# Twelve unused products in two stops of TensorE, ahead of the first job's scores

## The chip, the core and the metric

The kernel runs on one core of one Trainium2 chip. The metric is the device time of one execution in microseconds (us); the time given is the median of 8 runs. One execution was also profiled: the profile lists each instruction with its engine, start and length. TensorE (PE) does matrix products, with its weight loads listed apart (PEld); VectorE (DVE) does elementwise work, ScalarE (ACT) activations and copies, GpSimd (POOL) little here, and SyncE (SP) issues most of the DMA transfers.

## What is computed

Two layers, one after the other, in float32: a retention attention without softmax over 8 batches, 8 heads, 576 positions and 64 dimensions, and a gated feed-forward layer over its 4608 rows of 512.

```python
def _attn_ref(q, k, v):
    B, H, S, D_ = q.shape
    scale = 1.0 / np.sqrt(D_)
    scores = scale * np.matmul(q, k.transpose(0, 1, 3, 2))
    gamma = 1.0 - 2.0 ** (-5.0 - np.arange(H, dtype=np.float32))
    pos = np.arange(S)
    rel = pos[:, None] - pos[None, :]
    Dmat = np.where(rel >= 0, gamma[:, None, None] ** rel[None, :, :], 0.0)
    return np.matmul(scores * Dmat[None, :, :, :], v)

# x: the heads side by side, (4608, 512)
def _moe_ref(x, w_gate, w_val, w_out, rms_g):
    rms = np.sqrt(np.mean(x * x, axis=-1, keepdims=True) + 1e-06)
    xn = x / rms * rms_g
    g = xn @ w_gate
    silu = g * (1.0 / (1.0 + np.exp(-g)))
    return (silu * (xn @ w_val)) @ w_out
```

## The kernel before

The attention is cut into 32 jobs, one for each batch and pair of heads. A job handles its sequence in chunks of 64 positions. `scores` (L276) multiplies k and q inside a chunk, `states` (L296) multiplies k and v of a chunk into a 64 x 64 state for each head, `weigh` (L309) applies the causal mask to the scores on VectorE, `sums` (L323) adds the states up along the sequence on VectorE, `values` (L348) multiplies the weighted scores with v, and `carried` (L369) adds what the summed states give. `slot(j)` (L404) puts these in order: the values of job j-1, the scores and states of job j, its weighing and sums, and then the carried part of job j-1. The feed-forward part takes 384 rows at a time; the first two such units use plain products (`up_plain`, L602), the others a seven-product scheme for 2 x 2 blocks.

The order of every engine's instructions is written out by hand: the program runs under a manual schedule, so each engine does its instructions in the order in which the code below emits them, and semaphores hold it where data or a buffer is not yet there.

`start` (L905) is the part around the change. It makes the identity matrix and a tile of ones, runs six products of the ones with themselves into a bank named `warm` (L918 to L920), issues the first weight chunk and three tables on ScalarE's queue, and then the loads of the first eight jobs on SyncE's queue (`load_first`, L149, with `load_tails`, L189, for the last 64 positions). Then come `turn(0)`, `scale_v(0)` and three activations of the weights' conversion (`act(3)`), and a loop over eight jobs. In each turn of the loop stand `slot(j)`, `turn(j + 1)` for the next job, and `scale_v` of a later job, with pieces of the weight conversion between them.

`turn(j)` (L220) brings q and k of a job into transposed form. On TensorE it runs 8 products for q (L234, tile `turn_q`), 4 transposes for k (L228, `turn_k`) and 2 for the tails (L242, `turn_t`); on ScalarE it copies the results to `qT` and `kT` (L239, L248). `scale_v` (L259) scales the four pieces of v on ScalarE (L264). The scores need `qT` and `kT`, the states the scaled v.

The products write to banks of PSUM, of which the pool `banks` rotates five; `bank(name)` takes the next one. A float32 product appears in the trace as two matrix records and two weight loads; a transpose as one.

Of the kernel before, what the change touches and what calls it, by code (L numbers as in the profile page):

```python
# [14 lines left out]
P = 128  # L15
# [7 lines left out]
def _decay_tables(H, D):  # L23

    pairs = _gamma(H).reshape(H // 2, 2).T
    rows = np.repeat(pairs, D, axis=0)
    pos = np.arange(L)
    p = np.concatenate([pos, pos])  # L30
    gq = rows[:, :, None] ** (pos + L) / np.sqrt(D)
    t = pairs.T[None] ** -p[:, None, None], rows**L, gq, np.roll(gq, D, axis=0)
    return [np.ascontiguousarray(x).astype(np.float32) for x in t]


def _causal_table():

    return np.ascontiguousarray(np.tile(np.triu(np.ones((L, L), np.float32)), (2, 1)))
# [3 lines left out]
def kernel(  # L42
# [11 lines left out]
    nc = tc.nc  # L54
# [33 lines left out]
    def bank(name):  # L88
        return banks.tile([P, 512], F32, tag="b", name=name)
# [9 lines left out]
    ones = const.tile([P, P], F32, name="ones")  # L99
# [72 lines left out]
    def find_places():  # L172

        n = NFULL * 2 * D
        kv = {
            nm: [raw.tile([P, n], F32, tag=nm, name=f"first_{nm}_{i}", bufs=bufs) for i in range(bufs)]
            for nm, bufs in (("k", 4), ("v", 3))
        }
        other = raw.tile([P, S], F32, tag="qraw", name="first_k_7")[:, :n]
        sums = [ffn.tile([P, 3 * 2 * HU], F32, tag=t, name=f"first_{t}") for t in ("sums", "t1")]  # L180
        room = h_of[0].rearrange("p f t -> p (f t)")[:, 2 * NHP * 4 * P :]
        more = w_up[1][:, 8:].rearrange("p b f -> p (b f)")[:, 6 * DM :]
        return {
            "k": kv["k"] + kv["v"] + [other],
            "v": [t[:, i * n : i * n + n] for t in sums for i in range(2)]
            + [more[:, i * n : i * n + n] for i in range(3)] + [room],
        }
# [29 lines left out]
            out=t, in_=v[b, 2 * hp : 2 * hp + 2, NFULL * P :].rearrange("e p d -> p e d")  # L217
        )

    def turn(j):  # L220

        d = st[j]
        last = bank(f"turn_{j}_t")
        for nm in "qk":
            ps = bank(f"turn_{j}_{nm}")
            for c in range(NFULL):
                if nm == "k":
                    nc.tensor.transpose(  # L228
                        out=ps[:, c * P : c * P + P],
                        in_=d["k"][:, c].rearrange("p e d -> p (e d)"), identity=ident,  # L230
                    )
                    continue
                for e in range(2):
                    nc.tensor.matmul(  # L234
                        ps[side(e), c::NFULL], lhsT=d["q"][:, e, c], rhs=ident,
                        start=True, stop=True,
                    )
            t = d[nm + "T"] = att.tile([P, S], F32, tag=nm + "T", name=f"{nm}T_{j}")
            nc.scalar.copy(out=t[:, : NFULL * P], in_=ps)  # L239
        for i, nm in enumerate("qk"):  # L240
            o = slice(i * TAIL, i * TAIL + TAIL)
            nc.tensor.transpose(  # L242
                out=last[:, o], in_=d[nm + "t"].rearrange("p e d -> p (e d)"),
                identity=ident[:TAIL, :TAIL],
            )
        for i, nm in enumerate("qk"):
            o = slice(i * TAIL, i * TAIL + TAIL)
            nc.scalar.copy(out=d[nm + "T"][:, NFULL * P :], in_=last[:, o])  # L248
# [10 lines left out]
    def scale_v(j):  # L259
        d = st[j]  # L260
        hp = jobs[j][1]
        for e in range(2):
            for t in (d["v"][:, :, e], d["vt"][:, e]):
                nc.scalar.activation(  # L264
                    out=t, in_=t, func=AF.Copy, scale=gv[: t.shape[0], hp, e : e + 1]
                )
# [4 lines left out]
    def side(i):  # L271
        return slice(i * L, i * L + L)
# [489 lines left out]
    for g in range(NG):  # L762
        for m, src in enumerate((moe_w_gate, moe_w_val)):
            for half in range(2):
                n = (half * NH + 2 * g) * P
# [31 lines left out]
    def load_chunks(n, queue=nc.scalar):  # L797

        nonlocal n_loads
        while n_loads < min(n, len(chunks)) and waits_at.get(spare(n_loads)) is None:  # L800
            load_chunk(n_loads, queue)
            n_loads += 1
# [90 lines left out]
    def weights(n):  # L893

        for _ in range(n):
            next(steps, None)
# [8 lines left out]
    def start():  # L905

        h_of[0] = ffn.tile([P, NF, U], F32, tag="h", name="h_0")
        tables = list(zip((causal, gv, gc, gq, gx), (_causal_table(), *_decay_tables(H, D))))

        def table(i, queue):  # L910
            t, values_ = tables[i]
            src = nc.inline_tensor(values_, name=t.tensor.name + "_table")
            queue.dma_start(out=t, in_=src.ap())

        make_identity(nc, ident)
        nc.scalar.activation(out=tick, in_=mhalf[:1], func=AF.Silu)
        nc.vector.memset(ones, 1.0)
        warm = bank("warm")  # L918
        for _ in range(6):
            nc.tensor.matmul(warm[:, :P], lhsT=ones, rhs=ones, start=True, stop=True)  # L920
        first_places.update(find_places())
        load_chunks(1)
        for i in (1, 0, 2):
            table(i, nc.scalar)
        weights(3)
        for j in range(2 * NHP):
            load_first(j, {0: range(2), 1: range(2, H), NHP: range(H)}.get(j))
            if j == 1:
                table(3, nc.sync)
            load_chunks((1, 1, 1, 1, 2, 2, 2, 3)[j], nc.sync)  # L930
        table(4, nc.sync)
        nc.sync.dma_start(out=rms_g, in_=moe_rms_g.rearrange("(c p) -> p c", p=P))
        load_chunks(4, nc.sync)
        turn(0)
        scale_v(0)
        act(3)
        squares = []
        for j in range(2 * NHP):
            slot(j)
            if j + 1 < 2 * NHP:  # L940
                turn(j + 1)
            if squares:
                gather(*squares.pop())
            for i in ((1,), (2,), (3,), (4, 5), (6,), (7,), (), ())[j]:
                scale_v(i)
            if j:
                u, c = divmod(j - 1, NHP)
                squares.append((u, c, square(u, c)))
            act(1)
            if j == 5:  # L950
                norm_1(0)
            elif j == 6:
                norm_2(0)
            weights((2, 0, 0, 1, 1, 1, 1, 0)[j])
            if j == 4:
                gather(*squares.pop())
            elif j == 5:
                diagonals(0)
            act(1)
        gather(*squares.pop())  # L960
        load_qk(2 * NHP)
        load_kv(2 * NHP)
        made = combine_out()
        for m, g in [(m, g) for g in range(NG) for m in range(2)]:
            for u in range(2):
                weights_to(4 * g + 2 * m + 1)
                for i, _ in enumerate(up_plain(u, m, g)):
                    if not (u or m or g):
                        if i == 0:
                            values(2 * NHP - 1)  # L970
                            carried(2 * NHP - 1)
                            gather(1, NHP - 1, square(1, NHP - 1))
                        elif i == 1:
                            norm_1(1)
                        elif i == 2:
                            diagonals(1)
                        elif i == 3:
                            norm_2(1)
                    weights(2)
                    act(1)  # L980
                    if u and m and g == NG - 1:
                        weights_to(len(chunks))
                        next(made, None)
                    if i == 1:
                        weights_to(4 * g + 2 * m + 2)
        for _ in made:
            pass
        for blk, t in first_blocks.items():
            keep(blk, t)
        rest = across(1)  # L990
        next(rest)
        following(2 * NHP - 1)
        for i, _ in enumerate(rest):
            if i == 1:
                norm_0(2)
                differences(0)
            elif i == 2:
                norm_1(2)
                diagonals(2)
            elif i == 4:  # L1000
                norm_2(2)
        rest = across(0)
        next(rest)
        combine(1)
        slot(8, rest=False)
        following(8)
        for _ in rest:
            pass
        combine(0)
        slot(9)  # L1010
        following(9)
# [18 lines left out]
    with tc.manual_schedule():  # L1030
# [4 lines left out]
        for u in range(2, NU):  # L1035
# [11 lines left out]
            for i, _ in enumerate(rest):  # L1047
                if i == 0 and turns:
                    prepare_next(turns.pop())
                if i == 2:  # L1050
                    behind(u, 6)
                    at, n = SLOTS[u % 3]
# [33 lines left out]
```

## Time and profile before

| what | value |
|---|---|
| median of 8 runs | 1141.37 us |
| lowest and highest of them | 1139.93 and 1142.92 us |
| the profiled execution | 1140.38 us |
| its span, first to last instruction | 1138.6 us |
| mean granted TensorE clock | 0.997 |
| first job's q, turned on TensorE | 4.07 to 6.05 us |
| first job's k, turned on TensorE | 8.18 to 8.81 us |
| first job's scores begin | 10.05 us |
| last load in the chain of waits lands | 42.7 us |
| feed-forward products without a break from | 67.4 us |

Times inside the execution are counted from its first instruction. The page lists the busy time of each engine, the span in 40 slices, the queues, and the chain of work that ended last, followed back from the last instruction. A timeline lists instructions of one kind in order of time, merged where they follow each other, and in brackets the idle time of the engine ahead of them with what ended it. The granted clock is the share of TensorE's full clock that the records show; where there is no record yet, 1.0 is printed.

### The profile page before, as it was taken

The numbers are of one execution on the slowest core, as the hardware profiler recorded it, in microseconds if no ns is written. First come the engines' busy times: TensorE is split into PE (matmuls) and PEld (weight loads), VectorE is DVE, ScalarE is ACT, GpSimd is POOL, SyncE is SP. The second block draws the span as 40 slices with busy tenths as digits, with TensorE's granted clock in tenths as the row PEclk, the third lists the DMA queues.
The fourth block names the chain that finished last, engine by engine and source line by source line (L and its number), as shares of the span: only waits on it lengthen the run. The fifth ranks groups of instructions, "written<-read, shape, count | busy, mean of one in ns | idle before, by whom it ended". The sixth has DMA issues, their size and how long they took to land.

```text
span 1138.6 us, 24713 instructions
## 1 busy us (share of the span) xinstructions
PE 1116.4 (98%) x10470; PEld 1044.3 (92%) x10470; DVE 726.8 (64%) x1431; ACT 258.4 (23%) x508; POOL 39.7 (3%) x64
## 2 busy tenths in 40 slices
PE   7899999999999999999999999999999999999998
PEld 6655557999999999999999999999999999999998
DVE  5788868655675685375767676465676666446352
ACT  5546642012212211211221121121121220120210
POOL 0000000470000000000000000000000000000000
PEclk9999999999999999999999999999999999999999
DMA  8764336335364474053454555215436503303304
GB/s 203 215 184 148 111 126 197 62 64 135 96 136 98 112 160 143 1 121 88 106 125 60 132 133 120 114 35 118 119 79 141 142 20 97 126 1 100 124 1 111
DMA packets 292942, 125.40 MB, mean 110 GB/s; under 512 B 270432, under 2 KB 275808, under 8 KB 292832
## 3 DMA queue, kind: packets, MB, share of 16 engines
q1 hardware_dynamic: 282688, 107.66, 38.1%
q10 hardware_dynamic: 10144, 16.16, 4.4%
q8 instruction: 82, 1.34, 0.5%
q14 instruction: 28, 0.23, 0.1%
HBM read 108.83 MB, written 14.94 MB: 109 GB/s over the span
## 4 chain that ended last, share of the span: by engine, by line
PE 93%; SPq 3%; DVE 2%; DMA 1%; issue 1%; ACT 0%; DVEq 0%; POOL 0%; POOLq 0%
PE w L557 14%; PE x L557 14%; PE z L557 13%; PE up L614 10%; PE xo L688 8%; PE wo L688 8%; PE zo L688 8%; PE y L557 7%; PE yo L688 4%; SPq L165 2%; PE av L355 2%; PE s L284 1%; PE av L377 1%; PE s L304 1%; DVE sum L333 1%
## 5 line engine op out<-in xcount | busy, mean ns | idle before, releaser
L581 ACT COPY m<-x 128x384 f32<-128x384 f32 x60 | 28.7, 478 | 338.4 <-PE x L557 338.4
L688 PE MATMUL xo<-h,w_out 128*128 128x192 f32 x528 | 90.3, 328 | 0.0
L557 PE MATMUL w<-sums,w_val 128*128 128x192 f32 x480 | 88.7, 328 | 0.3
L557 PE MATMUL x<-x,w_val 128*128 128x192 f32 x480 | 88.8, 328 | 0.0
L557 PE MATMUL z<-x,w_gate 128*128 128x192 f32 x480 | 87.9, 326 | 0.7 <-DVE u L564 0.7
L557 PE MATMUL x<-x,w_gate 128*128 128x192 f32 x480 | 88.6, 328 | 0.0
L557 PE MATMUL z<-x,w_val 128*128 128x192 f32 x480 | 87.9, 326 | 0.0
L557 PE MATMUL w<-sums,w_gate 128*128 128x192 f32 x480 | 87.8, 326 | 0.0
L688 PEld LDWEIGHTS xo<-h,w_out 128*128 128x128 f32 x528 | 85.9, 190 | 0.6
L688 PE MATMUL wo<-h,w_out 128*128 128x192 f32 x504 | 85.3, 326 | 0.0
L564 DVE TENSOR_TENSOR u<-m,y 128x384 f32<-128x384 f32 x60 | 33.1, 552 | 79.0 <-PE y L557 79.0
L688 PEld LDWEIGHTS wo<-h,w_out 128*128 128x128 f32 x504 | 82.5, 190 | 0.0
L557 PEld LDWEIGHTS w<-sums,w_val 128*128 128x128 f32 x480 | 79.2, 190 | 2.7 <-DVE c L564 2.7
L557 PEld LDWEIGHTS z<-x,w_gate 128*128 128x128 f32 x480 | 79.6, 190 | 1.0 <-issue 1.0
L557 PEld LDWEIGHTS x<-x,w_gate 128*128 128x128 f32 x480 | 79.3, 190 | 0.5
L557 PEld LDWEIGHTS x<-x,w_val 128*128 128x128 f32 x480 | 79.2, 190 | 0.6
L557 PEld LDWEIGHTS z<-x,w_val 128*128 128x128 f32 x480 | 79.7, 190 | 0.0
L557 PEld LDWEIGHTS w<-sums,w_gate 128*128 128x128 f32 x480 | 79.6, 190 | 0.0
L564 DVE TENSOR_TENSOR h<-u,w 128x384 f32<-128x384 f32 x60 | 33.1, 551 | 69.5 <-PE w L557 69.4
L576 ACT ACTIVATE h<-h 128x384 f32<-128x384 f32 x90 | 47.0, 522 | 89.6 <-DVE h L564 89.6
L614 PE MATMUL up<-x,w_gate 128*128 128x384 f32 x192 | 63.3, 488 | 0.9 <-DVE x L526 0.7
L614 PE MATMUL up<-x,w_val 128*128 128x384 f32 x192 | 62.4, 486 | 0.0
(187 smaller groups left out, 1766.3 us busy)
## 6 DMA issues: line engine op xcount, KB each, us to landing
w_out<-w_blocks SPq DMA_DIRECT2D x70, 768.0 KB, 5.1
out_dram<-o SPq DMA_DIRECT2D x368, 24.0 KB, 1.6
qraw<-in_q_dram SPq DMA_DIRECT2D x96, 72.0 KB, 2.7
kraw<-in_k_dram SPq DMA_DIRECT2D x96, 72.0 KB, 2.7
k<-in_k_dram SPq DMA_DIRECT2D x48, 128.0 KB, 2.9
v<-in_v_dram SPq DMA_DIRECT2D x48, 128.0 KB, 2.9
w_out<-in_moe_w_gate_dram ACTq DMA_DIRECT2D x5, 1024.0 KB, 5.8
w_out<-in_moe_w_out_dram ACTq DMA_DIRECT2D x3, 1024.0 KB, 4.8
```

Of the source, the lines that this page charges most:

```text
L165: nc.sync.dma_start(out=t[:, :, e], in_=src[b, 2 * hp + e, : NFULL * P].rearrange("(c p) d -> p c d", p=P),)
L284: nc.tensor.matmul(s[side(odd), e, i * L : i * L + L], lhsT=d["kT"][side(e), c * L : c * L + L], rhs=d["qT"][side(e), c * L : c * L + L], ...
L304: nc.tensor.matmul(o[side(e)], lhsT=d["k"][side(odd), i, e], rhs=d["v"][side(odd), i, e], start=True, stop=True,)
L333: nc.vector.scalar_tensor_tensor(out=t[:, c], in0=t[:, c - 1], scalar=gc[:, hp : hp + 1], in1=part, op0=ALU.mult, op1=ALU.add,)
L355: mm = nc.tensor.matmul(av[odd][column(j, odd, e), i * L : i * L + L], lhsT=d["v"][side(odd), i, e] if c < NC - 1 else d["vt"][:, e], rhs= ...
L377: mm = nc.tensor.matmul(av[odd][column(j, odd, e), i * L : i * L + L], lhsT=d["sum"][side(e), c - 1], rhs=d["qT"][side(e), c * L : c * L + L],
L557: nc.tensor.matmul(ps[:, i * HU : i * HU + HU], lhsT=w_up[m][:, 2 * blk + c, cut], rhs=t_of[u][blk][:, c], start=(start and i == c == 0), ...
L564: nc.vector.tensor_tensor(out=o, in0=a, in1=pairs_of(ps), op=ALU.add)
L576: nc.scalar.activation(out=o, in_=c, func=AF.Silu)
L581: nc.scalar.copy(out=s1, in_=pairs_of(x_))
L614: nc.tensor.matmul(ps[:, :U], lhsT=w_up[m][:, 4 * half + c, i * P : i * P + P], rhs=x_of[u][:, c], start=(c == 0), stop=(c == NHP - 1),)
L688: nc.tensor.matmul(ps[:, i * HU : i * HU + HU], lhsT=a[:, c, i * P : i * P + P], rhs=rhs[:, c], start=(start and i == c == 0), stop=False, ...
```

## The change

The six products at the start become a call of a new helper, `warm_up(n)`, which emits n products of the tile of ones with itself into the same bank. `turn` gets an argument `waits` with two counts: so many such products ahead of the transposes of k, and so many after the transposes of the tails. Only `turn(0)` passes counts, 8 and 4; all other calls use 0 and 0. The results of these products are not read. The emitted order on the other engines is the same.

```diff
-    def turn(j):
+    warm_of = {}
+
+    def warm_up(n):
+
+        if not warm_of:
+            warm_of[0] = bank("warm")
+        for _ in range(n):
+            nc.tensor.matmul(
+                warm_of[0][:, :P], lhsT=ones, rhs=ones, start=True, stop=True
+            )
+
+    def turn(j, waits=(0, 0)):
+
 
         d = st[j]
         last = bank(f"turn_{j}_t")
         for nm in "qk":
+            if nm == "k":
+                warm_up(waits[0])
             ps = bank(f"turn_{j}_{nm}")
...
                 identity=ident[:TAIL, :TAIL],
             )
+        warm_up(waits[1])
         for i, nm in enumerate("qk"):
...
-        warm = bank("warm")
-        for _ in range(6):
-            nc.tensor.matmul(warm[:, :P], lhsT=ones, rhs=ones, start=True, stop=True)
+        warm_up(6)
         first_places.update(find_places())
...
-        turn(0)
+        turn(0, (8, 4))
         scale_v(0)
```

## The prediction

> **What bounds the kernel now.** I read the page's busy shares first, then the chain of waits over the first 66 us, then the timeline of the first 20 us engine by engine, and last the clock by windows. Busy shares with the slices say that TensorE is the bound of almost the whole run, and that only the start leaves it room:
>
> ```profile
> PE 1116.4 (98%) x10470; PEld 1044.3 (92%) x10470; DVE 726.8 (64%) x1431; ACT 258.4 (23%) x508; POOL 39.7 (3%) x64
> ...
> PE   7899999999999999999999999999999999999998
> ```
>
> From 67.4 us on the chain is TensorE almost alone, so an earlier end needs an earlier arrival there. The chain of waits (start, length, what) tells how the start is paced:
>
> ```profile
> 3.69 5.52 DMA first_sums<-in_v_dram
> 9.22 0.41 SPq L165
> ...
> 38.61 4.09 DMA w_val<-in_v_dram
> 42.72 0.75 ACT w_val L264 x2
> 43.47 0.42 ACT sq L439
> 43.92 0.56 DVE sq L449
> ...
> 67.40 5.40 PE up L614 x16
> ```
>
> SyncE issues loads from 0.73 to 38.6 us, a last one lands at 42.7, then VectorE works almost without a gap to 66 us, then TensorE. No product of the first job stands in it. The timeline around the two stops (start, length, engine, line, operation, out<-in, count, idle time before and what ended it):
>
> ```profile
> 4.07 1.98 PE L234 MATMUL turn_q<-ident,h 128*64 128x128 f32 x16
> 8.18 0.63 PE L228 MATMUL turn_k<-ident,first_k 128*128 128x128 f32 x4 [2.13 <-DMA first_k<-in_k_dram]
> 8.74 0.33 PE L242 MATMUL turn_t<-ident,w_val 64*128 64x64 f32 x2
> 9.40 0.59 ACT L239 COPY kT<-turn_k 128x512 f32<-128x512 f32 x1
> 10.05 1.34 PE L284 MATMUL s<-qT,kT 64*64 64x64 f32 x40 [0.98 <-ACT kT L239]
> 12.45 0.89 DVE L316 SCALAR_TENSOR_TENSOR ret<-s,causal 128x320 f32<-128x320 f32 x2 [3.16 <-PE last L304]
> 17.41 0.35 ACT L264 ACTIVATE w_val<-w_val,gv 64x64 f32<-64x64 f32 x1 [0.93 <-DMA w_val<-in_v_dram]
> 18.21 0.62 PE L304 MATMUL s<-first_sums,first_k 64*64 64x64 f32 x25 [1.35 <-ACT first_sums L264]
> 18.92 0.89 DVE L316 SCALAR_TENSOR_TENSOR ret<-s,causal 128x320 f32<-128x320 f32 x2 [0.78 <-PE last L304]
> ```
>
> TensorE stops twice, 2.1 us for the first k and about 1 us for the copies of ScalarE. The last three lines matter most: at 17.41 ScalarE, at 18.21 TensorE and at 18.92 VectorE all stand idle in the second job for one load. The windows (stretch, length, busy PE, granted clock, DMA share, GB/s) show what the stops cost:
>
> ```profile
> 6.32:9.73 3.41, 0.89 (x6) 0.99 0.98 151
> 9.73:13.15 3.42, 3.10 (x80) 0.51 1.08 237
> 13.15:16.56 3.41, 2.97 (x95) 1.00 1.13 196
> 37.04:40.45 3.41, 1.99 (x43) 1.00 0.81 195
> ```
>
> After a stretch with 0.89 us of work the clock is halved for one stretch of 3.41 us, and the first scores and states fall into it. A stretch with 1.99 us of work kept the clock.
>
> **What the Trainium skill says.** "TensorE: Matmul & The Clock Gate", Part 1, gives the gate half and full rate alone, decided per free-running window of 3413 ns: an idle one halves the clock, a busy one restores it. The trace agrees: the slow stretch is 3.41 us at 0.50, behind a nearly idle one of the same length. The same page's specification table calls the queues of ScalarE and VectorE strict FIFO; here the copies and scalings of ScalarE do run in the order written, and the argument below rests on it. "DMA: Bandwidth & Descriptors", Why small descriptors are slow, explains dear small packets; here the first 62 us move 28241 packets, 23180 of them under 512 B, and the DMA engines are near full at 8 to 18 us.
>
> **The change, part by part.** It adds 12 products and removes and moves nothing else; the orders of VectorE, ScalarE, GpSimd and SyncE are the same with the same waits. No DMA is added. The products read a constant and write their own bank, and carry no wait.
>
> Price of one: the six at the start are 12 records in 2.93 us at half rate. Taking one record's latency, about 0.46 us, off leaves 11 steps of 0.224 us, so 0.45 us a product, 0.22 us at full clock (an estimate by the halving). The start does run at half rate although the page prints 1.0 there: its turn_q takes 1.98 us, the later ones at full clock 1.09 us.
>
> First stop, 8 products, 16 records. TensorE can issue from about 5.7 us (turn_q's end at 6.05 less the latency). Up to 6.32 at half rate: 0.62/0.224 = 2.8 records. The other 13.2 at 0.112 = 1.5 us: the last ends near 8.1. The first k lets TensorE go at 8.15, so they fit, to within 0.1 us. Behind them wait turn_k and turn_t, and behind those ScalarE's kT copy at 9.40, for which turn_k was ready at 8.81: 0.59 us more of cover. Cost zero; without cover it would be their 1.5 to 3.6 us (all at full, all at half rate).
>
> Second stop, 4 products, 8 records of 0.112 = 0.9 us from about 8.9 us, ended by about 10.0; the scores start at 10.05. Cost zero, 0.1 us at most.
>
> What it gives locally: the stretch from 6.32 to 9.73 holds about 0.9 + 1.7 + 0.8 = 3.4 us instead of 0.89, so the clock stays up from 9.73 to 13.15. The scores take 0.78 us as at 15.93 instead of 1.34. The states can't follow at once: the second head's v is scaled on ScalarE until 11.25 (10.74 + 0.51). From there the second job's states took 0.69 us at full clock (18.21 to 18.90), so they end at about 11.97 instead of 12.42. VectorE weighs the first job at 12.0 instead of 12.45: 0.45 us earlier. The second turn_q saves another 0.34 us (1.43 less 1.09).
>
> Where that goes: TensorE's values of the first job wait at 15.41 for ScalarE's copy of the second qT, which stands behind three 1.15 us activations of the weights (11.38 to 14.89), none of them waiting for TensorE. From 15.41 TensorE is where it was. ScalarE goes on to 16.48, and stands until the v tails of the second job, issued by SyncE at 12.20, land at 17.4. Hence states at 18.21, and VectorE's weighing at 18.92, unmoved: its 0.45 us turns into idle time, 0.78 + 0.45 = 1.23 us before that line. After it all five engines are where they were. If the load came earlier by the whole 0.93 us, ScalarE would be the next late one, not TensorE. Sum: 0 - 0 + 0 = 0 us on the end, against the profiled execution's 1140.38 us (span 1138.6 and 1.8 around it), which lies 1.0 us under the median. So 1141.4 for the median.
>
> One side effect: with earlier work the stretch 13.15 to 16.56 empties. Left in it are some turn_k and turn_t (0.6 us), four products of the values (0.3) and 15.41 to 16.56 (1.15): about 2.0 us, and 1.99 us kept the clock above. I take no loss; a halved stretch to 19.97 with its 2.06 us of work would cost 1 to 2 us locally.
>
> **The rivals.**
> Gain carried (faster). A halved clock over 3.10 us of work loses 1.55 us; if the start were paced by TensorE after all in most executions, all of that would be won: 1139.8; with two stretches halved in other executions, 3.1 us: 1138.3. For it: the records do show the loss, and one execution says little on the window's phase in others. Against: the idle times at 17.41, 18.21 and 18.92, and again VectorE's 0.96 us at 35.09 and ScalarE's 1.57 us at 37.50, both for loads.
>
> Late first scores (slower). The extra products hold up turn_k, if the array is still at half clock over the first stop. Then 16 x 0.224 = 3.6 us from 5.7 us end at 9.3, turn_k at about 10.3, kT's copy 0.9 us late; turn_t to 10.4, then 8 x 0.224 = 1.8 us, so scores at 12.3 instead of 10.05 and the first weighing 2.3 us late. 0.78 us idle before 18.92 takes some: 1.5 us late there, 1142.9 if no later load wait absorbs it, and 2.3 us if the first doesn't either: 1143.7. It decides from where the products end after 8.7 us (8.15 + 0.59). For it: the fit is tight and the phase free. Against: a clock record of 1.0 from 6.32, and turn_k at 8.18 as quick (0.63 us) as at 20.78 (0.66).
>
> No change of clock. In the execution's phase the gate halves anyway, or had not halved: 1141.4 too, since the products are hidden.
>
> **How the numbers follow.** Forecast 0.71, gain carried 0.15, late scores 0.08, no change of clock 0.06. What this kernel's measurement can tell from no change is about 0.2%, 2.3 us. Of the gain's 0.15 I put 0.09 beyond that, since only the two-stretch value passes it, and 0.02 of the forecast for drift; of the late scores 0.05 and 0.01 for drift: faster 0.11, slower 0.06, same 0.83. Range: the runs before span 1139.9 to 1142.9; reaching to the one-stretch gain (1139.8) and the absorbed lateness (1142.9), trimmed to what two in ten leave out: 1139.3 to 1142.7.
>
> **What would show it.** Right: clock 1.0 from 9.73 to 13.15, scores still at about 10.05 but 0.8 us long, the first weighing near 12.0, TensorE's wait at 15.4 and the second weighing at 18.9 unmoved, the second's idle time up to about 1.2 us, the up products still at 67.4. Wrong: turn_k later than 8.3, scores later than 10.2, a halved stretch after 13.15, or a second weighing before 18.5.

## The result and the profile after

The changed kernel takes 1146.95 us (median of 10 runs, 1145.49 to 1148.73) against 1141.13 us (28 runs). The ratio is 1.0051, 95% interval 1.0042 to 1.006: 5.8 us slower, outside the range given. The profiled execution took 1146.99 us, its span is 1145.2 us.

TensorE's busy time and the clock row of the page of the changed kernel:

```profile
PE 1123.5 (98%) x10494; PEld 1050.7 (92%) x10494; DVE 726.9 (63%) x1431; ACT 258.4 (23%) x508; POOL 40.1 (3%) x64
...
PEclk8899999999999999999999999999999999999999
```

TensorE has 24 matrix records more (10494 against 10470) but is busy 7.1 us longer, and the first two slices of the clock row, which showed 9 (90% of full clock or more), show 8. The chain of waits of the same execution (start, length, what) shows where the time sits:

```profile
17.57 1.01 PE s L319 x25
...
20.40 1.90 PE turn_q L248 x16
...
32.71 3.28 issue
...
73.37 5.40 PE up L629 x16
```

Where the chain before ran through SyncE's issues, it now runs through TensorE: `turn_q` of the third job takes 1.90 us where it took 1.09, and for 3.28 us TensorE runs nothing ("issue" is time in which the engine waits for nothing that the profile shows). The unbroken feed-forward products begin at 73.37 us instead of 67.40: of the 6.6 us between the two profiled executions, 6.0 are lost before that.

The timeline of the two stops and of VectorE's weighings says when (the columns as before):

```profile
5.98 2.32 PE L227 MATMUL warm<-ones 128*128 128x128 f32 x16
8.14 0.60 PE L242 MATMUL turn_k<-ident,first_k 128*128 128x128 f32 x4
8.93 1.16 PE L227 MATMUL warm<-ones 128*128 128x128 f32 x8
10.02 0.81 PE L299 MATMUL s<-qT,kT 64*64 64x64 f32 x40
11.87 0.89 DVE L331 SCALAR_TENSOR_TENSOR ret<-s,causal 128x320 f32<-128x320 f32 x2 [2.60 <-PE last L319]
18.72 0.89 DVE L331 SCALAR_TENSOR_TENSOR ret<-s,causal 128x320 f32<-128x320 f32 x2 [1.15 <-PE last L319]
26.05 0.89 DVE L331 SCALAR_TENSOR_TENSOR ret<-s,causal 128x320 f32<-128x320 f32 x2 [3.16 <-PE s L319]
32.18 0.89 DVE L331 SCALAR_TENSOR_TENSOR ret<-s,causal 128x320 f32<-128x320 f32 x2 [1.97 <-PE s L319]
43.77 0.89 DVE L331 SCALAR_TENSOR_TENSOR ret<-s,causal 128x320 f32<-128x320 f32 x2 [5.10 <-PE s L319]
```

Up to the second job all is as predicted, even a little early. The weighings of the third to fifth job stood so before:

```profile
24.14 0.89 DVE L316 SCALAR_TENSOR_TENSOR ret<-s,causal 128x320 f32<-128x320 f32 x2 [1.05 <-PE s L304]
29.51 0.89 DVE L316 SCALAR_TENSOR_TENSOR ret<-s,causal 128x320 f32<-128x320 f32 x2 [1.20 <-PE s L304]
36.51 0.89 DVE L316 SCALAR_TENSOR_TENSOR ret<-s,causal 128x320 f32<-128x320 f32 x2 [0.72 <-PE s L304]
```

Now they are 1.9, 2.7 and 7.3 us late. Two things lie there. The windows of the changed kernel (stretch, length, busy PE, PEld, DVE, ACT, POOL, clock, DMA share, GB/s) show two stretches at half clock, each twice as long as the one before and in places where TensorE is needed:

```profile
13.40:16.81 3.41, 2.18 (x81) 1.77 (x80) 3.13 (x8) 2.96 (x8) 0.09 (x1) 1.00 0.64 140
16.81:23.64 6.83, 6.07 (x84) 5.22 (x84) 4.61 (x15) 1.78 (x5) 0.00 (x0) 0.50 0.99 230
33.60:37.00 3.40, 1.01 (x22) 0.94 (x23) 1.99 (x8) 0.00 (x0) 0.00 (x0) 1.00 1.09 224
37.29:44.12 6.83, 5.96 (x133) 4.92 (x129) 1.73 (x5) 5.39 (x14) 0.09 (x1) 0.50 1.04 240
```

The first follows the stretch that the earlier work left emptier, the second follows the long gap. And the gaps put down to "issue" have a place of their own, which shows when TensorE's records are counted: matrix records, weight loads and the semaphore instructions between them, in order of their start, the first as number 0. A gap "after record 1217" stands ahead of the record with that number.

### The profile page after: what moved, and what is told of

Read it like the earlier page. It is cut to its first block, busy times and chain, and to the rows that moved or that the text cites. A ratio compares the mean times of both kernels' runs of the same rounds, so it can differ in the third digit from the quotient of the medians.

```text
span 1145.2 us, 24760 instructions
## 1 busy us (share of the span) xinstructions
PE 1123.5 (98%) x10494; PEld 1050.7 (92%) x10494; DVE 726.9 (63%) x1431; ACT 258.4 (23%) x508; POOL 40.1 (3%) x64
## 4 chain that ended last, share of the span: by engine, by line
PE 96%; issue 1%; DVE 1%; DMA 1%; SPq 1%; ACT 1%; POOL 0%; DVEq 0%; POOLq 0%; ACTq 0%
PE x L572 14%; PE w L572 14%; PE z L572 14%; PE up L629 11%; PE xo L703 8%; PE wo L703 8%; PE zo L703 8%; PE y L572 7%; PE yo L703 4%; PE av L370 2%; PE av L392 2%; PE s L299 2%; PE s L319 1%; PE ms L490 1%; PE turn_q L248 0%
```

## What the gaps are

The page's queue list has this queue in both kernels (packets, MB, share of 16 engines' span):

```profile
q8 instruction: 82, 1.34, 0.5%
```

That is about 16 KB a packet. TensorE has about 21100 records; divided by 82 that is 257 a packet. In the kernel before, TensorE stops twice for over a microsecond:

```profile
32.51 0.65 PE L234 MATMUL turn_q<-ident,h 128*64 128x128 f32 x7 [1.43 <-issue]
38.46 1.02 PE L377 MATMUL av<-qT,sum 64*64 64x64 f32 x26 [1.78 <-issue]
```

The records behind these gaps have the numbers 1217 and 1473, which are 256 apart; a third, shorter gap stands ahead of record 2497, five times 256 on. The changed kernel stops at the same three numbers, and at 961 and 1729, which are on the same grid, though its program is there some 48 records behind (the 24 matrix records and their weight loads). In the 14 traces of this case, between 22 and 66 us, TensorE's timelines put 55 idle times down to "issue", of 0.25 to 4.05 us: every one stands at a number of this grid, 193 and a multiple of 256.

Worked out from the two traces and from those of the experiments below, for the block that begins at record 1217 (us; record 961 opens the block before it; the packet is the last that landed before record 1217; a gap is counted from the start of one record to that of the next, and so is up to 0.3 us longer than the idle time in the views):

```
kernel                record 961   packet    packet   record 1217   gap ahead
                      begins       begins    landed   begins        of 1217
before                27.95        29.77     30.89    32.51         1.71
changed               29.70        33.24     34.35    35.99         3.50
e4 (changed again)    28.26        32.29     33.19    34.55         3.50
e12 (cut, held)       28.48        33.70     34.93    36.44         3.07
e1 (shift only)       27.16        28.76     30.23    31.81         1.85
e3 (wide)             31.01        34.25     35.54    37.16         3.23
e9 (wide, held)       27.71        28.36     29.73    31.56         1.04
e6 (load early)       30.18        31.64     32.83    34.28         0.17
```

In every gap of over 0.4 us at a border, a packet of that queue has landed 1.2 to 1.9 us before TensorE goes on. In the crowded first 66 us a packet begins 0.2 to 6.1 us after the record that opens the block before (in one trace a single one begins earlier). Later, where the records take longer, it begins between 7 us ahead of that record and 4 us behind it, and mostly lands long before it is needed. So TensorE's instructions come in blocks of 256, about one block ahead; where a block's records run off faster than the next block arrives, TensorE stands. The Trainium skill says this in "Runtime: NRT & Kernel Launch", Instruction fetch mechanics: an engine's instructions are refilled in blocks of 16 KiB, 256 of them, over a DMA queue of its own. It calls the cost of a border mostly hidden; the 3.50 us here differ, and the measurement decides. The grid belongs to the count of instructions; how long a gap gets is another matter. `e3_wide` has the record count of the kernel before, and still 3.23 us ahead of record 1217. The prediction never asked this.

## The experiments

All ratios are to the kernel before; edits are to the changed kernel unless said otherwise. Theory A is the moved block borders, theory B the clock. The forecasts count matrix records alone: 24 of them are 48 in the count above, with their weight loads.

**e1_shift_only**: the 24 records without the filled stops.

```diff
-        warm_up(6)
+        warm_up(4)
+        small(14)
...
-        turn(0, (8, 4))
+        turn(0)
```

`small` is a new helper that emits 64x64 products of the ones.

> The two stops are left empty as in the kernel before; the 12 added products stand in the group at the very start instead, as small 64x64 ones (4 of the six big ones and 14 small), so TensorE's instruction count ahead of the scores is that of the changed kernel, 24 records more than before, with hardly more work. Theory A (TensorE's instructions come in blocks of 256, both traces show gaps after records 1217, 1473 and 2497; the added records move these borders to other places of the program, where TensorE runs out of instructions and waits for the next block): about as slow as the changed kernel, +3 to +6 us against before, with a gap over 1 us after record 1217. Theory B (the clock: two halved stretches of 6.83 us in the changed kernel, set off by the products in the stops): about the time before, within 1 us.

Measured 1145.65 us, ratio 1.0034 (1.002 to 1.0048), +3.9 us on the ratio. The gap after record 1217 is there, 1.85 us, with 2.34 after 1473 and 2.05 after 2497. Two thirds of the loss come without a product in the stops; B alone is out. The added products themselves are not what costs: they take 3.25 us at the start, but the first four weighings of its profiled execution are only 0.1 to 0.2 us late. The fifth is 2.9 us late (39.45 against 36.51):

```profile
38.70 0.60 PE L329 MATMUL s<-w_val,first_v 64*64 64x64 f32 x11 [2.12 <-issue]
39.45 0.89 DVE L341 SCALAR_TENSOR_TENSOR ret<-s,causal 128x320 f32<-128x320 f32 x2 [4.01 <-PE s L329]
```

Border 1473 has nearly the same idle time as before (2.12 against 1.78 us), at nearly the same moment (38.70 against 38.46 us). But before it stood in the products that follow the fifth job's states (`av<-qT,sum`), after VectorE had its input; With 48 records more ahead of it, the program reaches the border earlier: it stands inside the states (`s<-w_val,first_v`), and VectorE waits for them. So it matters where in the program a border falls, and not only how long TensorE stands there. (A stretch at half clock begins at 38.5 us too; how the 2.9 us divide isn't separated.)

**e2_first_stop**: `turn(0, (8, 0))`, the first stop alone.

> Only the first stop is filled (8 products, 16 records); the second is as before. Theory A: the borders move by 16 records instead of 24, so a loss of the same kind, somewhere between +1 and +6 us, with the gap again after record 1217. Theory B: the clock isn't held up through the second stop, so the halved stretches fall elsewhere; +0 to +3 us.

Measured 1144.79 us, ratio 1.0028 (1.0016 to 1.004). Gaps of 1.89, 1.80, 1.81, 0.70 and 2.25 us after 1217, 1473, 1985, 2241 and 2497. The interval fits both theories, so it tells only that the first stop alone suffices for over half of the loss.

**e3_wide**: the same work in fewer products.

```diff
-                warm_of[0][:, :P], lhsT=ones, rhs=ones, start=True, stop=True
+                warm_of[0][:, :cols].rearrange("p (a b) -> p a b", b=P), lhsT=ones,
+                rhs=ones.unsqueeze(1).to_broadcast([P, cols // P, P]), start=True, stop=True,
...
-        warm_up(6)
+        warm_up(3, 256)
...
-        turn(0, (8, 4))
+        turn(0, (2, 1))
```

In `turn` the products now have 512 columns.

> Both stops are filled for the same time as in the changed kernel, with fewer and wider products: 3 of 256 columns at the start for 6 of 128, 2 of 512 in the first stop for 8, 1 of 512 in the second for 4. TensorE then has exactly as many records ahead of the scores as in the kernel before, and the clock is kept up as in the changed kernel. Theory A: the loss is gone, -1 to +1 us against before. Theory B: as slow as the changed kernel, +4 to +6 us.

Measured 1143.18 us, ratio 1.0019 (1.0006 to 1.0032), between the two. More than half of the loss is gone with the borders back in place, about 2 us stay, and the runs are wide (1139.13 to 1149.7). The nine runs with a mean clock of 0.997 or more have a median of 1141.2 us, the six under 0.995 one of 1146.6 (the kernel before: 1140.4 and 1142.4). The windows of its profiled execution:

```profile
14.95:18.36 3.41, 2.00 (x79) 1.54 (x78) 2.64 (x3) 1.93 (x7) 0.09 (x1) 1.00 1.10 221
18.36:25.18 6.82, 6.19 (x84) 5.22 (x84) 3.85 (x14) 1.77 (x5) 0.00 (x0) 0.50 0.88 203
```

The kernel before had a stretch with as little work at much the same place (busy PE, clock, DMA share, GB/s), and kept its clock in the one that followed:

```profile
16.56:19.97 3.41, 2.06 (x80) 1.00 0.88 210
```

With the stops filled, the halved stretch has moved from 9.7 us, where loads cover it, to 18.4 us. So there is a second term.

**e4_again**: the changed kernel once more.

> The changed kernel once more, for a second trace. Theory A: the long gap after record 1217 (3.5 us in the first trace) is there again, whatever the clock does, and the time is +4 to +7 us. Theory B: two halved stretches of about 6.8 us again at much the same places, and the time follows the mean clock.

Measured 1147.73 us, ratio 1.0052 (1.0033 to 1.0071). The gap after 1217 is 3.50 us again. The halved stretches are others: 3.41 us each, at 16.1, 53.6 and 63.9 us. So that gap repeats; the lengths of the others (0.86 and 2.06 us after 1473) and the clock differ from one execution to the next. The trace line at border 1217, of the first execution and of this one:

```profile
35.99 0.62 PE L392 MATMUL av<-qT,sum 64*64 64x64 f32 x14 [3.28 <-issue]
```

```profile
34.55 0.62 PE L392 MATMUL av<-qT,sum 64*64 64x64 f32 x14 [3.28 <-issue]
```

**e9_hold**: e3_wide with one 512-column product after the second job's turning, and 2 products of 384 columns at the start, so that the count is kept.

```diff
-                turn(j + 1)
+                turn(j + 1, (0, 0 if j else 1))
```

> As e3_wide (stops filled by wide products, record count ahead of the second job as before), with one more 512-column product after the turning of the second job, paid for by 2 products of 384 columns at the start instead of 3 of 256, so that the count is that of before from the second job's values on. e3_wide had no moved borders and was still 2 us slow on the median; its clock fell to half at 18.4 us, after the stretch in which TensorE waits for the second job's loads. Theory A with the clock as a second term: if the extra product keeps that stretch busy enough, the halved stretch at 16 to 25 us goes and the time is -1 to +1 us against before. If the second term isn't the clock, or one product isn't enough, +1.5 to +3 us as e3_wide.

Measured 1141.38 us, ratio 0.9991 (0.9976 to 1.0005): the loss is gone. Filling the stops, then, costs nothing if the count is kept and the clock held. 11 of its 12 runs have a mean clock of 0.997 or more. Windows of its profiled execution at the place where e3_wide fell:

```profile
15.09:18.50 3.41, 2.89 (x108) 2.00 (x112) 2.64 (x3) 2.54 (x8) 0.09 (x1) 1.00 0.98 221
18.50:21.91 3.41, 3.11 (x69) 2.50 (x60) 2.83 (x10) 1.17 (x4) 0.00 (x0) 1.00 0.95 222
```

**e12_hold_cut**: the changed kernel with `turn(j + 1, (0, 0 if j else 4))`: the work of e9_hold in 128-column products.

> The changed kernel with four more products of 128 columns after the turning of the second job: TensorE does the same extra work at the same four places as in e9_hold, cut into 128-column products instead of 256 to 512, so that the two differ in the number of instructions alone (24 records more ahead of the scores, 32 from the second job's values on). Theory A: the clock is held as in e9_hold (0.997 to 0.998) and the loss of the moved borders remains, +3 to +6 us against before, with a gap over 1.5 us after record 1217. If the count doesn't matter: the time of e9_hold, -2.5 to +0.6 us.

Measured 1145.49 us, ratio 1.004 (1.0026 to 1.0054), with a gap of 3.07 us after 1217. Against e9_hold it has the same extra columns at the same places in more instructions, and is 4.1 us slower on the medians. The pair isn't clean: its clock wasn't held as expected (0.993 to 0.997, mean 0.9948 against 0.9977), and the difference of 0.0029 of 1141 us is up to 3.3 us of TensorE time. At 0.995 to 0.997 its three runs take 1144.5 to 1145.5 us, the three of e9_hold 1141.45 to 1143.31: some 2 us are left for the number of instructions, an estimate from six runs.

**e6_load_early** asks what makes a block late: the changed kernel with the 1 MB load of a weight chunk one job earlier.

```diff
-            load_chunks((1, 1, 1, 1, 2, 2, 2, 3)[j], nc.sync)
+            load_chunks((1, 1, 1, 2, 2, 2, 2, 3)[j], nc.sync)
```

> The changed kernel with one edit: the 1 MB load of the second weight chunk is issued one job earlier on SyncE's queue (with the fourth job's loads, not the fifth's). Theory A, with the wait of an instruction block put down to the transfers issued ahead of it: the block that starts at record 1217 no longer begins 3.5 to 4 us after it was asked for but about 2 us, the gap after record 1217 falls from 3.5 us to under 2.5, and the block before (record 961) waits longer instead; the time may fall by up to 2 us or stay. If the wait has nothing to do with that load, the gap after 1217 stays at 3.5 us.

Measured 1147.21 us, ratio 1.004 (1.0026 to 1.0054). The gap after 1217 falls to 0.17 us, that ahead of record 961 grows from 1.01 to 2.12 and the wait of its packet, from record 705 on, from 1.89 to 3.05 us. The wait moves with the load. The time stays slow: 4.6 us on the ratio, within its interval of the changed kernel's 5.8. In the timeline of this kernel the stop after 1217 is gone, and those at 961 and 1473 are there:

```profile
30.18 0.27 PE L256 MATMUL turn_t<-ident,w_val 64*128 64x64 f32 x1 [1.85 <-issue]
41.70 0.51 PE L319 MATMUL s<-w_val,first_v 64*64 64x64 f32 x12 [2.40 <-issue]
```

**e11_before_load_early**: the same edit in the kernel before.

> The kernel before with the load of the second weight chunk issued one job earlier, as in e6_load_early. There the long wait moved from the block of record 1217 to that of record 961. In the kernel before, the block of 961 is asked for at 23.1 us, just ahead of where the load then stands, so it should escape; the block of 1217 should come without a gap (1.7 us before), that of 1473 (2.0 us) is open. Theory A: -2 to 0 us. If the wait isn't set by that load: 0, with the gap after 1217 still 1.7 us.

Measured 1142.74 us, ratio 1.001 (0.9999 to 1.002): a miss. The gap after 1217 goes (0.07 us) and that after 1473 shrinks (1.46), but the packet for 961 was caught all the same (it begins 3.69 us after record 705, gap 1.64), and 1985 and 2497 have gaps of 1.18 and 2.12 us.

**e8_minus8**: stops empty, `warm_up(2, 384)` at the start, 8 records less.

> The stops empty as before; the six products of 128 columns at the start become two of 384, the same work with 8 records less ahead of everything. Theory A: the borders move the other way, so the time changes though nothing is added: -2 to +4 us. Theory B and any theory of added work: the time of before within 0.7 us.

Measured 1144.07 us, ratio 1.0031 (1.0019 to 1.0043), 3 us slower with nothing added. Gaps of 0.47, 0.68, 2.62 and 1.22 us after 705, 1217, 1473 and 1729. The clock has a part: its mean over these runs is 0.993, that of the kernel before 0.9955, and the four runs at 0.995 to 0.997 have a median of 1143.6 us. How much is borders and how much clock isn't separated by this run alone.

**e7_shift64**: 32 small products in the first stop, `turn(0, (32, 0))` with `small` for `warm_up`.

> 32 small 64x64 products (64 records) in the first stop, none in the second. Theory A says that the time follows where the borders fall and not how much is added: gaps again at records 1217, 1473 and so on, in a different pattern, a time anywhere from -1 to +6 us, and not 64/24 times the loss of the small products (which would be +10 us). A rival by which each added record costs the same says +10 us.

Measured 1149.72 us, ratio 1.0071 (1.005 to 1.0092), above A's range and nearer to the rival's. The experiment was badly sized: the small products take 3.94 us (the timeline's `warm` group of 64), so k's turning begins at 9.78 instead of 8.15 us. Still the first weighing is only 0.6 us late (13.08) and the second at 18.94 as before; then come gaps of 1.95, 4.27, 1.73, 1.10 and 1.45 us after 961, 1217, 1729, 1985 and 2241. The loss arises behind these borders, but A had no means to say its size.

**e5_late** and **e10_late_bank**: 12 small products ahead of the first seven-product output stage, at 189 us.

> The stops are left empty and the start is as before; 12 small 64x64 products (24 records) are added ahead of the first seven-product output stage instead, far behind the crowded loads of the first 66 us. Theory A (block borders): a border moved there costs nothing, since the next block lands long before it is needed; the time is that of before plus the products' own 0.7 us, 0 to +1.2 us. Rival (24 more records cost time wherever they stand): +3 us or more.

Measured 1152.99 us, ratio 1.0096 (1.0081 to 1.0111), far above A's range. It is no control: the products use the bank of the first ones, which so stayed taken for 190 us. With a bank of their own most of the excess goes:

```diff
+        late = bank("late")
+        for _ in range(12):
+            nc.tensor.matmul(
+                late[:L, :L], lhsT=ones[:L, :L], rhs=ones[:L, :L], start=True, stop=True
+            )
         rest = across(1)
```

> e5_late once more with a bank of its own at the late place. In e5_late the bank of the first products stayed taken for 190 us, so the first eight jobs and the plain products had four banks to rotate instead of five, and its +11 us say nothing on the added records. Theory A: 12 small products there cost their own 0.7 us, 0 to +1.5 us. Rival (24 more records cost time wherever they stand): +3 us or more.

Measured 1143.96 us, ratio 1.0021 (1.001 to 1.0032), +2.4 us, between the two forecasts. The chain of waits has the products themselves:

```profile
189.27 1.54 PE late L1005 x24
```

So 1.54 us are their own (64 ns a record, not the 30 assumed), and the feed-forward products began 1.0 us late in this execution, ahead of anything added. Of the 2.4 us, 0.9 are left for all else. The interval reaches to 3.7 us, so the rival's 3 us are made unlikely and not ruled out. Borders are not quite free there either: after record 2600 the trace of the kernel before has gaps of 0.74 and 0.96 us at two of them (5057, 5569), this one 1.03, 0.91 and 0.97 us at three (7361, 7873, 10945).

Put together (us). The loss is that of the timed runs on the ratio, with their number and mean clock (for the kernel before, those measured beside the experiments). The other columns are of the one profiled execution of each kernel: its gaps of over 0.3 us at borders up to record 2497 added up, its time at half clock in stretches that begin between 14 and 70 us, and how late its unbroken feed-forward products begin, against 67.40 us. `e5_late`, with its bank taken, is left out.

```
kernel       loss   runs   mean clock   gaps at borders   half clock   feed-forward late
before        0     113      0.9955           4.2             0             0
e9_hold      -1.0    12      0.9977           6.4             3.4           1.6
e11          +1.1    14      0.9949           6.4             6.8           3.0
e3_wide      +2.2    20      0.9961           5.3            10.2           5.0
e10          +2.4    12      0.9958           4.8             3.4           1.0
e2           +3.2    20      0.9945           8.5            10.2           6.8
e8           +3.5    20      0.9930           5.0            10.2           3.8
e1           +3.9     7      0.9964           7.7             6.8           4.4
e12          +4.6     5      0.9948           7.5            13.7           6.8
e6           +4.6     5      0.9950           6.0            10.2           5.0
changed      +5.8    10      0.9947           7.5            13.7           6.0
e4           +5.9     4      0.9950          10.1            10.2           7.6
e7           +8.1     7      0.9959          10.9             3.4           7.4
```

The losses follow the gaps only roughly: e9_hold has 2.2 us more of them than the kernel before and loses nothing, while e6 and e8 lose far more than the gaps they add. Within the profiled executions two terms go together. A least-squares fit (an estimate, over these 12 against the kernel before) puts the late begin of the feed-forward products at 0.81 us for each us of added gaps and 0.29 us for each us at half clock, 1.0 us for one stretch of 3.41. It meets all 12 to within 1.2 us, 0.7 in the root mean square; with gaps alone or half clock alone that is 1.8 and 1.9.

The profiled execution of the kernel before had no halved stretch after 14 us and so flatters it. In the timed runs the clock tells the two kernels apart far less: 0.9947 and 0.9955 is under 1 us of TensorE time. At 0.997 and above the changed kernel's four runs (with e4_again) have a median of 1145.9 us, the 28 of the kernel before 1140.4: at the same clock 5.5 us of the loss are still there.

## Why the prediction was wrong

The local part held. The eight products ended at 8.30 us (forecast 8.1) and k's turning began at 8.14 (8.15); the scores began at 10.02 (10.05) and took 0.81 us (0.8); the first weighing was at 11.87 (12.0), the second at 18.72 (18.9) behind 1.15 us of idle time (1.2). The clock was full from 9.73 to 13.15. What was to be won there was indeed lost in the wait for the second job's loads.

The step that failed is "After it all five engines are where they were." TensorE was not: its instructions had 24 matrix records and as many weight loads more behind them, and the borders of its blocks lay elsewhere in the program, some of them ahead of products that VectorE waits for. The description of the change, that it "adds 12 products and removes and moves nothing else", counted work and waits and not instructions. The term this left out is about 4 of the 5.8 us: e1_shift_only has it alone (3.9 us), with a mean clock no lower than before. e9_hold, with the stops filled and the count kept, loses nothing, and e12_hold_cut, with the count raised again, loses 4.6 us, though part of that is clock. The profile before showed it: two idle times of 1.43 and 1.78 us put down to "issue", 256 records apart. The prediction quoted idle times for loads and passed over those two.

The second failure is a size. "I take no loss; a halved stretch to 19.97 with its 2.06 us of work would cost 1 to 2 us locally" named the right place, and the loss taken should have been about 2 us: e3_wide has 2.2 us with the borders in place, and e9_hold, which fills just that stretch, has none. A halved stretch after 13.15 us was among the prediction's own signs of being wrong, and it came, at 16.81. The ground for taking none, that a stretch with 1.99 us of busy time had kept its clock, didn't hold: 2.18 us in the changed kernel and 2.00 us in e3_wide lost it, where 2.06 us before kept it. The busy column alone doesn't tell which stretch loses the clock; what does was not found.

The rivals fared no better. "Late first scores" had the right sign and the wrong mechanism: nothing was late at the first scores. And a start paced by loads was taken as cover for all that TensorE does; it covered the first 19 us, but TensorE itself became late from 24 us on, which no rival had.

Open are the exact rule by which a block is delayed (the 1 MB load moves the wait in e6_load_early, but packets far from it wait 3 to 5 us too), why a halved stretch comes where it does, and how the losses of e8_minus8 and e7_shift64 divide between borders, clock and, in e7, the products themselves.

## What to carry to other kernels

Where TensorE runs many short instructions while the DMA queues are full, look for idle time put down to "issue" at counts that are multiples of 256 apart: here each was the border of an instruction block, and in every long one the block had come late. An edit that changes the number of instructions moves those borders, and can cost microseconds far behind the edit (some 25 us later here) without adding work that matters, above all where a border comes to stand ahead of something that another engine waits for. To fill a stop, take few wide instructions rather than many narrow ones, keep the count, and compare the traces at the borders and at the halved stretches. A clock kept up in one stretch is worth nothing if loads pace that stretch, and it may fall in the next one, where it counts.

## What was not expected of the hardware

A block of TensorE's instructions took up to 8.9 us from the record 256 ahead of it to its own first record (e7_shift64, record 1217), and TensorE went on only 1.2 to 1.9 us after the packet had landed. Small products of 64 x 64 took 62 to 64 ns a record when all of them used the same quarter of the array (3.94 us for 64, 1.54 us for 24), where the scores, which alternate, take 0.81 us for 40. The small products also all write one place, so which of the two counts isn't tested. The same changed kernel had its halved stretches at 16.8 and 37.3 us in one execution and at 16.1, 53.6 and 63.9 us in another.
